# A delta-rule attention and mixer kernel: two of the eight transfers of the first K unit issued by GpSimd as its first instructions

## The chip, the cores and the metric

The kernel runs on one core of a Trainium2 chip. A core has TensorE (PE, matrix products, results in PSUM), VectorE (DVE), ScalarE (ACT), GpSimd (POOL) and SyncE (SP), which here only issues transfers. ScalarE and GpSimd issue transfers too. All transfers between the device's memory and the on-chip memory (SBUF) are carried by 16 DMA engines. The metric is the device time of one execution in microseconds (us); the smaller the better.

## The reference

Inputs are q, k, v of shape (4, 8, 768, 48), that is batch, heads, sequence and head dimension, beta of shape (4, 8, 768), and the mixer's weights U (768, 32), V (32, 768), w_ch1 (384, 1536) and w_ch2 (1536, 384), all float32. First a delta rule runs over the sequence, for each batch and head:

```
k_n = k / (norm(k) + 1e-6);  state = 0
for t: y[t] = q[t] @ state
       state += beta[t] * outer(k_n[t], v[t] - k_n[t] @ state)
```

Then the heads are laid side by side as x (4, 768, 384), and a mixer follows: `u = x + (x^T U V)^T`, `out = u + relu(u @ w_ch1) @ w_ch2`.

## The kernel before

The recurrence is cut into chunks of 64 steps. A *unit* is half of one batch's sequence for all 8 heads, 6 chunks each; there are 8 units. Within a chunk the rule becomes a triangular system built from the products of K with itself (Gram products), the norms of K and beta. A unit is worked as follows: K is loaded into a *slot* of SBUF (two slots, used in turn), TensorE turns it (line 233), ScalarE and VectorE copy it from PSUM (432 and 434 for the first unit, 437 for later ones), TensorE makes the Gram products (461), these are copied into the slot (473, 476, 480), VectorE lays their diagonal blocks out (521), ScalarE takes the square root for the norms (394, after loading a table), VectorE combines norms and beta (397 to 406) and then substitutes in a long series of small operations (530, 532). After that come the states and the outputs of the attention, and then the mixer, whose large matrix products (1264, 1358) take most of the kernel's time. Mixer weights are loaded and combined during the first units (858, 877, 883, 886).

The order of the work on all engines is written out by hand. Each part of the work is a Python generator that yields what it needs and which engine it uses next; `begin` numbers the parts in the order they are begun, and the string ORDER lists those numbers: each token lets one part issue its next step. Parts 0 and 1 are the two calls of `load` for the K of unit 0, 2 and 37 and such are further loads. Part 0 issues on SP the four heads of lower number, part 1 on ScalarE the four of higher number; within each part the transfers go by `s` = 0 to 3. A pair of `s` (0 and 1, then 2 and 3) forms one *half* j of the heads, and each half is turned by TensorE in one go once all of its four transfers have landed. One transfer is 64 x 6 pieces of 192 bytes, 72 KB.

An engine works its instructions in their order; a waiting instruction holds up all that stand behind it. Waits are set by the framework from what the instructions read and write. Transfers carry semaphores of their own, eight for those of SP and ScalarE together and eight for those of GpSimd, which are handed out in turn; so a transfer waits until the one eight before it in that group has landed.

Ahead of the ordered part the kernel sets up constants. On GpSimd these are the identity (`ident`, used by every turn on TensorE), a triangular mask (`upper`, `mask_u`) and two memsets of parts of the slots (275). Behind them on GpSimd's queue come, in this order: one Q transfer, two K transfers of unit 1, the two transfers of beta (363), the mixer's U (858), and more of K and Q. Beta is turned by TensorE at line 374 and copied by ScalarE at 378; in TensorE's order line 374 stands behind the Gram products of unit 0 and ahead of the turn of unit 1's K, and in ScalarE's order the copy of that turn (437) stands ahead of the table load and the square root of unit 0's norms (394).

Of the kernel before, what the change touches and what calls it, by code (L numbers as in the profile page):

```python
# [6 lines left out]
FP32 = mybir.dt.float32  # L7
# [16 lines left out]
def kernel(ctx: ExitStack, tc: tile.TileContext, q: bass.AP, k: bass.AP, v: bass.AP, beta: bass.AP, moe_U: bass.AP, moe_V: bass.AP, moe_w_ch1: bass.AP, moe_w_ch2: bass.AP, out: bass.AP):  # L24
# [59 lines left out]
    297 71 207 61 297 301 208 61 297 301 61 61 208 298.2 297 303 298 207 68 304q 208 298 70 71 304 44 207  # L84
# [1367 lines left out]
```

## Time and profile before

| | |
|---|---|
| median of 3 runs | 576.2 us (574.73 to 580.31) |
| the profiled execution | 572.55 us |
| its span | 570.8 us |
| granted TensorE clock, mean | 0.976 |
| TensorE busy | 537.4 us, 94% of the span |
| VectorE busy | 417.4 us, 73% |
| ScalarE busy | 243.1 us, 43% |
| GpSimd busy | 130.0 us, 23% |
| mean transfer rate over the span | 68 GB/s |

The span is the profiled execution without 1.75 us around it. Busy times of engines lie beside each other and do not add up to the span. "SPq", "ACTq" and "DVEq" are the sequencers that issue, an issue of a transfer by GpSimd counts as busy POOL. A row of the timeline has the start, the length, the engine, the line, the operation, what it writes and reads, how often, and in brackets the idle time before it and what ended that. A row of transfers has what is moved, the issuing queue, the count, the size, and the median time from issue to landing.

### The profile page before, as it was taken

Reading aid. Unit: us, or ns where it says so; the run is one execution under the profiler, and the core shown is the slowest. Engines: PE = TensorE matmul, PEld = TensorE weight load, DVE = VectorE, ACT = ScalarE, POOL = GpSimd, SP = SyncE. Lnnn points to the kernel's source line nnn. Section 1 sums busy time; section 2 is a strip of 40 time slices with the busy share of each in tenths; the row PEclk is TensorE's granted clock in tenths of the full one; section 3 lists DMA queues with packets and bytes.
Section 4 is the critical chain, followed back from the end, with each engine's and each line's share of the span. In section 5 each row is a group of like instructions: output and inputs, shape, how many; then the busy total and the mean of one; then the engine's idle time right before and its main releaser. Section 6 shows DMA issues by size and latency. Waiting matters only on the chain.

```text
span 570.8 us, 24657 instructions
## 1 busy us (share of the span) xinstructions
PE 537.4 (94%) x10965; PEld 454.7 (80%) x10965; DVE 417.4 (73%) x1062; ACT 243.1 (43%) x525; POOL 130.0 (23%) x229
## 2 busy tenths in 40 slices
PE   4776989999999999999999999999999999999997
PEld 4675877669789688789879977988879888656997
DVE  5798976799897439999887889999653356656542
ACT  3786885452435453155236433632452341336100
POOL 8061064552201453131044133400000000000000
PEclk9997579999999999999999999999999999999999
DMA  9957766542200353250033233310000000100001
GB/s 144 184 124 224 229 179 138 117 100 53 72 3 17 78 126 85 53 103 3 3 78 83 66 86 64 81 27 2 17 4 2 31 2 1 41 2 0 15 14 57
DMA packets 70763, 38.67 MB, mean 68 GB/s; under 512 B 56768, under 2 KB 67776, under 8 KB 70656
## 3 DMA queue, kind: packets, MB, share of 16 engines
q1 hardware_dynamic: 62368, 25.87, 19.2%
q0 software_dynamic: 6688, 10.92, 8.2%
q8 instruction: 86, 1.41, 1.1%
q10 hardware_dynamic: 1600, 0.30, 0.3%
q14 instruction: 21, 0.17, 0.1%
HBM read 32.34 MB, written 4.72 MB: 65 GB/s over the span
## 4 chain that ended last, share of the span: by engine, by line
PE 82%; DVE 8%; ACT 3%; DMA 2%; SPq 2%; issue 2%; DVEq 0%; ACTq 0%
PE P L1358 26%; PE P L1264 14%; PE P L221 9%; PE P L997 7%; PE P L461 4%; PE P L1041 2%; PE P L1088 2%; PE P L780 2%; PE P L739 2%; PE P L752 2%; DMA slot<-in_k_dram 2%; PE P L1186 2%; PE P L687 1%; PE P L1060 1%; PE P L694 1%
## 5 line engine op out<-in xcount | busy, mean ns | idle before, releaser
L1264 PE MATMUL P<-ut,w_sb 128*128 128x256 f32 x360 | 83.1, 385 | 0.2 <-ACT hs L1234 0.2
L1358 PE MATMUL P<-w_sb,hs 128*128 128x192 f32 x456 | 80.4, 330 | 0.0
L1358 PEld LDWEIGHTS P<-w_sb,hs 128*128 128x128 f32 x456 | 73.9, 190 | 3.9 <-issue 1.8
L1264 PEld LDWEIGHTS P<-ut,w_sb 128*128 128x128 f32 x360 | 66.7, 190 | 9.6 <-ACT hs L1234 0.3
L532 DVE TENSOR_TENSOR xt<-xt,prod 128x112 f32<-128x112 f32 (+21 forms) x200 | 64.2, 321 | 5.1
L530 DVE TENSOR_TENSOR prod<-gs,xt 128x112 f32<-128x112 f32 (+21 forms) x200 | 63.7, 318 | 4.3
L1304 DVE TENSOR_TENSOR X<-X,P 128x192 f32<-128x192 f32 x85 | 29.4, 347 | 42.9 <-PE P L1358 42.1
L344 POOL DMA_DIRECT2D slot<-in_k_dram x48 | 27.7, 582 | 95.5 <-PE P L780 60.9
L1234 ACT ACTIVATE hs<-P 128x512 f32<-128x512 f32 x42 | 24.9, 598 | 56.2 <-PE P L1264 43.6
L677 ACT COPY X<-P 64x192 f32<-64x192 f32 x96 | 30.1, 313 | 35.1 <-PE P L694 30.4
L1358 PE MATMUL P<-w_sb,S 128*128 128x192 f32 x240 | 41.3, 328 | 0.0
L1358 PEld LDWEIGHTS P<-w_sb,S 128*128 128x128 f32 x240 | 39.0, 190 | 0.8 <-DVE X L1304 0.6
L221 PE MATMUL P<-ut,w_sb 64*64 64x256 f32 x576 | 39.0, 383 | 0.2
L653 ACT COPY slot<-zz 32x384 f32<-32x384 f32 x64 | 34.5, 540 | 8.4 <-DVE zz L536 5.4
L461 PE MATMUL P<-slot 48*64 48x64 f32 x1536 | 33.1, 243 | 4.0 <-ACT slot L437 3.0
L461 PEld LDWEIGHTS P<-slot 48*64 48x64 f32 x1536 | 30.3, 156 | 7.4 <-ACT slot L437 3.6
L344 POOL DMA_DIRECT2D slot<-in_q_dram x48 | 27.2, 572 | 32.7 <-DVE slot L450 14.4
L657 POOL MEMSET slot<- 32x384 f32 x32 | 13.8, 431 | 90.9 <-PE P L628 89.8
L788 DVE TENSOR_TENSOR s<-s,P 128x192 f32<-128x192 f32 x40 | 14.0, 351 | 22.6 <-PE P L780 16.3
L982 DVE TENSOR_TENSOR slot<-slot,P 128x384 f32<-128x384 f32 x36 | 18.6, 551 | 15.8 <-PE P L997 15.5
L1358 PE MATMUL P<-w_sb,slot 128*128 128x192 f32 x180 | 29.9, 326 | 0.0
L1358 PEld LDWEIGHTS P<-w_sb,slot 128*128 128x128 f32 x180 | 29.4, 190 | 0.3
(205 smaller groups left out, 1059.1 us busy)
## 6 DMA issues: line engine op xcount, KB each, us to landing
w_sb<-in_moe_w_ch_dram SPq DMA_DIRECT2D x14, 384.0 KB, 5.2
out_dram<-X SPq DMA_DIRECT2D x22, 192.0 KB, 2.8
slot<-in_k_dram SPq DMA_DIRECT2D x36, 72.0 KB, 3.7
slot<-in_k_dram POOLq DMA_DIRECT2D x32, 72.0 KB, 3.3
slot<-in_v_dram SPq DMA_DIRECT2D x32, 72.0 KB, 3.0
slot<-in_v_dram POOLq DMA_DIRECT2D x32, 72.0 KB, 2.7
X<-in_moe_w_ch_dram SPq DMA_DIRECT2D x6, 384.0 KB, 4.6
wide<-in_moe_w_ch_dram SPq DMA_DIRECT2D x4, 384.0 KB, 5.8
```

The lines of the kernel that those rows point to most:

```text
L221: nc.tensor.matmul(to[half(g)], w[half(r), half(g)], x[half(r)], start=start, stop=stop, skip_group_check=True)
L344: queue.dma_start(out=in_pairs(n, int(name == 'q'), j)[quarter(2 * par + y), :, g, 0:cols.stop - cols.start], in_=of[:, :, cols])
L461: nc.tensor.matmul(p_g[half(g ^ par * i), par, c], kq[rows, c, j, 0, half(g)], kq[rows, c, j, i, half(g)], start=True, stop=True)
L530: nc.vector.tensor_tensor(out=prod, in0=gb[:, :, j, j + 1:, None].to_broadcast([128, split, w, m]), in1=xb[:, :, j:j + 1, 0:m].to_broadcas ...
L532: nc.vector.tensor_tensor(out=xb[:, :, j + 1:, 0:m], in0=xb[:, :, j + 1:, 0:m], in1=prod, op=ALU.subtract)
L653: nc.scalar.copy(pg[quarter(i), :, at, :, a:a + BK], thirds(h)[quarter(i)].rearrange('p r (c j) t -> p r c j t', j=2))
L677: nc.scalar.copy(x[half(c % 2), c // 2, 4 * D * g:4 * D * (g + 1)].rearrange('p (j r d) -> p r j d', r=2, d=D), states(p_y)[half(g)])
L997: nc.tensor.matmul(banks[x], w1_sb[:, 4 * a[0] + e, a[1]] if isinstance(a, tuple) else w1_mixes[a][:, e], tokens(*t) if isinstance(t, tupl ...
L1234: nc.scalar.activation(hs[:, fs[0]:fs[1] + 1:fs[1] - fs[0]], p_f, ACTF.Relu)
L1264: nc.tensor.matmul(p_f[:, x], w(x, t), ut[:, t], start=t == 0, stop=t == KT - 1)
L1304: nc.vector.tensor_tensor(out=to, in0=to, in1=p, op=ALU.add)
L1358: nc.tensor.matmul(to, of[0], of[1], start=of[2], stop=of[3], skip_group_check=True)
```

## The change

The tiles of the slots are made before the constants, and GpSimd issues two transfers ahead of everything else it does: `s` = 3 of both groups of heads, the last head of each group of four for unit 0's K. In `load`, unit 0's K skips `s` = 3, and the second half counts as issued as soon as `s` = 2 is. So SP and ScalarE issue three transfers each rather than four. The new helper `fetch` only holds the call of the transfer that stood in `load` before. In ORDER the two tokens of the removed steps are gone; all its other tokens are the same, in other line breaks. The order of the instructions on TensorE and VectorE is the same as before.

```diff
     ORDER = """
-    0 1 0 149 1 0 1 22 0 1 37 37 21 2 36 2 2 14.0 36 147 36 37 21 216 216 39 38 22 15.1 38 39 148 37 217.2
+    0 1 0 149 1 0 1 22 37 37 21 2 36 2 2 14.0 36 147 36 37 21 216 216 39 38 22 15.1 38 39 148 37 217.2 36 218
...
     def quarter(i, size=BK):
         return slice(BK * i, BK * i + size)
+    slots = [const.tile([128, 9792], FP32, name=f'slot{i}') for i in range(2)]
+
+    def fetch(queue, t, n, name, h):
+        b, hf = divmod(n, NU)
+        queue.dma_start(out=t, in_=name[b, h, hf * UC * L:(hf + 1) * UC * L, :].rearrange('(c t) d -> t c d', t=L))
+    for g in range(2):
+        fetch(nc.gpsimd, slots[0][half(g), 0:1536].rearrange('p (c s d) -> p c s d', c=UC, s=4)[:, :, 3, 0:D], 0, k, 4 * g + 3)
     ident = const.tile([128, 128], FP32, name='ident')
     make_identity(nc, ident)
...
-    slots = [const.tile([128, 9792], FP32, name=f'slot{i}') for i in range(2)]
...
             for s in range(1, 4, 2) if name == 'z' else range(4):
+                if (n, name, s) == (0, 'k', 3):
+                    emitted((name, n, g, 1))
+                    continue
                 to = dict(k=s, q=s, v=s % 2 * 2 + s // 2, z=s // 2)[name]
                 yield op(e)
-                queue.dma_start(out=t[half(1 - g if name == 'z' or (name == 'k' and n >= NU and s % 2) else g), :, to, 0:D], in_=src[b, 4 * g + s, hf * UC * L:(hf + 1) * UC * L, :].rearrange('(c t) d -> t c d', t=L))
+                fetch(queue, t[half(1 - g if name == 'z' or (name == 'k' and n >= NU and s % 2) else g), :, to, 0:D], n, src, 4 * g + s)
```

More of the change, by code (lines that the diff above doesn't have):

```diff
@@ new lines @@
+    337 205 206 9 9.0 349 350.1 205 206 348 9 9.0 206 205 348 338q 348 9 205 206 338 9.2 338 338 9 338 351.0 9.2
+    352 350 9 162 350 339q 350 9.2 339 9 351 339 9.1 80 89 90 89 90 89 90 89 90 81 81 80 80 339 351 87 9 90 9.2
+    336 339 90 9 89 334.1 90 334 356 9.2 89 90 357 340 9 89 351 83 334 357 355.2 83 9.0 91 92 340 9 89 92 91 92
+    341 359 88 91 334 88 87 9.0 355 354.1 9 88 87 9.0 341 9 84 354 84 354 357 210 209 355 342 355 354 210 209
+    354 333 342 92 210 360.0 363 9.2 353.1 361 9 9.2 344q 353 9 353 364 9.2 353 344 353 85 360 9 365.1 344 9.2
@@ new lines @@
+    360 344 360 9 78 78 364 9.0 344 9 78 364 9.2 366.0 343 365 9 9.2 365 365 368 207 208 9 78 367 9.1 208 207 78
+    369.2 78 85 345q 207 208 208 207 345 85 85 88 91 85 9 85 209 9.1 345 85 345 85 9 209 85 85 366 85 9.1 85 345
+    366 9 366 85 85 372.0 9.1 370 369 9 85 9.1 85 346 9 85 369 85 369 371 85 372 107 97 107 106 107 106 107 106
+    106 97 97 362.1 373 106 107 372 85 372 85 358.2 210 106 85 362 107 106 180.0 362 107 106 85 87 107 85 85 346
+    85 180 85 85 85 180.1 85 347 180 85 375 358 180.0 358 376 98 180 181.1 85 374.2 85 377q 98 181 104 377 388.0
[6 rows of a table added]
@@ new lines @@
+    102 102 391 387 391 102 409 102 10.0 410 182q.2 10 102 10.0 394 411 10 394 182 102 102 411 102 102 102 422.0
+    423 102 408.1 10.2 102 412q 10 102 10.2 102 422 412 10 422 102 10.2 422 102 424.0 10 412 102 10.2 408 412
+    408 10 102 412 102 10.1 426.2 425 424 10 102 10.1 424 413q 102 424 10 102 10.0 102 413 209 210 10 102 10.1
[7 rows of a table added]
+    449 119 10 10.0 450 446 440 450 451q 446 10 446 119 119 10.1 451 119 10 119 462.0 119 10.2 451 119 451 10
+    119 119 10.1 119 462 451 119 10 447.2 119 464 119 10.1 119 112 452 10 119 119 447 447 452 119 119 119 463.1
@@ new lines @@
+    465 10.2 119 453 119 462 462 119 119 10 453 119 119 10.0 466 468.2 463 10 119 10.0 463 454q 463 119 10 467
+    10.1 119 454 211 212 10 119 10.0 454 468 211 212 469.1 10 468 162 10.0 212 376 468 454 10 162 211 212 10.2
+    119 454 409 10 119 471.0 211 470 10.2 119 469 119 455 119 119 119 455 119 10 119 456 119 472 119 469 119 469
+    456 119 119 119 10.2 119 473 119 10 119 471 141 141 141 140 141 140 131 140 140 131 458q 471 132 471 132
+    183.1 474 467 119 119 131 458 183 140 141 119 183.2 162 141 140 458 458 119 141 138 183 138 141 458 119 138
@@ new lines @@
+    139 119 183q.0 119 140 139 474 119 138 139 478 183 184.1 474 476.2 140 139 119 119 475.0 477 476 119 119 476
[3 rows of a table added]
+    490 142 121 136 481.2 136 142 501 481 136 491 136 481 136 481 136 483 136 491 136 136 136 136 184q.0 136 136
+    486.2 129 184 492 486 502 162 486 492 136 129 493 503 136 136 493 504 504 504 11.1 505 136 494 11 136 136
+    136 494 136 136 136 495 136 136 136 11.0 506.2 136 495 506 136 506 11 136 136 11.1 508 136 510.2 185.0 11
+    507 11.1 509 497 11 185 136 136 136 11.1 136 497 509 136 136 11 511 11.0 512 513.1 510 11 509 11.0 510 498q
@@ new lines @@
+    136 11 496 510 11.0 498 136 11 136 11.2 136 514.0 498 513 136 498 136 513 513 11 136 11.1 136 498 11 136 136
+    11.2 136 185.1 11 136 515 11.2 136 185 514 11 499 516 514 136 514 136 136 136 136 136 499 136 518 136 523
+    522 500 519 522 519 522 522 11.2 524 523.1 11 523 517.0 523 522 11.2 525q 522 11 525 536.1 11.2 525 525 11
+    521 520 11.2 525 11 517 11.2 537 536 214 213 213 213 520 526q 214 517 517 214 526 214 536 214 536 521.0 214
+    521 213 526 520 526 214 520 520 214 520 11 526 521 521.1 521 538 11.2 539.0 521 527q 11 521 11.2 527 11 11.1
@@ L157 @@
+    527 527 11 11.2 527 11 540.1 214 11.2 213 541 539 214 539 528 214 539 214 542 542 528 542 529 543 11 529 530
+    544 530 532 545 532 547 546 546 546 533 531 548 533 549 11.0 550 523.2 11 523 11.0 523 540 534q 11 523 540
+    540 11.0 534 11 551.2 11.1 534 534 11 11.0 534 11 213 11.1 552.0 554 11 554 11.1 551 11 551 553 11.1 551 552
+    555.2 11 552 552 11.1 11 11.0 535q 11 556.1 11.0 535 11 11.0 555 558 11 557 556 213 558 215.0 215 566 556
[12 rows of a table added]
     """
```

30 lines of the change are left out of this document (2 added, 28 removed), and 136 rows, old and new, of the table ORDER.

## The prediction

> **What bounds the kernel now.** I read the page first: the share of each engine and the chain that ended last. Then the chain in order of time for the first 20 us, since the change touches only the start; then the timeline and the landings of the single transfers there.
>
> ```profile
> span 570.8 us, 24657 instructions
> PE 537.4 (94%) x10965; PEld 454.7 (80%) x10965; DVE 417.4 (73%) x1062; ACT 243.1 (43%) x525; POOL 130.0 (23%) x229
> PE 82%; DVE 8%; ACT 3%; DMA 2%; SPq 2%; issue 2%; DVEq 0%; ACTq 0%
> 18.00:42.00 24.00, 18.28 (x535) 16.52 (x538) 22.90 (x72) 18.97 (x38) 9.57 (x14) 1.00 0.68 151
> ```
>
> TensorE is busy 94% of the span and is 82% of the chain. A change of two transfers alters none of its work; it can only move the moment from which everything runs. The last row (columns: stretch, length, busy time and count of PE, PEld, DVE, ACT, POOL, then clock, DMA share, GB/s) says whether a move of the start is passed on: from 18 to 42 us VectorE is busy 22.90 of 24 us with the substitution, which starts when the norms are ready. There is no slack there, so a shift of the norms is a shift of what follows. The question is therefore when the norm of line 394 can run.
>
> ```profile
> 1.61 0.86 SPq L351
> ...
> 2.53 0.64 SPq L351
> ...
> 3.21 4.68 DMA slot<-in_k_dram
> 7.89 0.14 issue
> 8.02 1.00 PE P L233 x12
> 9.02 2.81 PE P L461 x96
> ...
> 13.26 0.80 ACT slot L480
> 14.06 0.79 ACT slot L437
> ...
> 14.87 1.28 ACT L394
> ...
> 16.16 0.26 ACT norm L394
> ...
> 18.07 0.13 DVE xt L406
> ```
>
> This chain (start, length, what) runs over SP's issues to the last transfer of the first unit's K (issued at 3.21, landed at 7.89) over its second turn on TensorE (8.02), the Gram products, their copies and the table load to the norm at 16.16, and on to the seed of the substitution (line 406). Taken by itself it says that K earlier by x makes the norm earlier by x. The timeline shows a second path that ends at the same place.
>
> ```profile
> 5.58 1.00 PE L233 MATMUL P<-ident,slot 64*128 64x64 f32 x12 [5.58 <-DVE even L283]
> ...
> 11.72 1.46 PE L374 MATMUL P<-ident,X 16*64 16x16 f32 x24
> ...
> 13.11 0.91 PE L233 MATMUL P<-ident,slot 64*128 64x64 f32 x12
> ...
> 14.05 0.80 ACT L437 COPY slot<-P 128x768 f32<-128x768 f32 x1
> ```
>
> The copy of line 437 stands ahead of the norm's table load on ScalarE. It reads the turn of the other slot's K, which TensorE ends at 13.11 + 0.91 = 14.02, and TensorE does that only after the turn of beta (line 374, 11.72 to 13.1). So line 437 is released at 14.02 by TensorE and at 14.06 by ScalarE: two paths within 0.04 us. The beta path hangs on two transfers of GpSimd's queue, and the change puts two others ahead of them.
>
> **The change part by part.** The order of the instructions on TensorE and VectorE is the same in both kernels; SP and ScalarE each issue three K transfers in place of four, GpSimd issues two more ahead of all its work.
>
> ```profile
> 0.83 3.01 SPq L351 DMA_DIRECT2D slot<-in_k_dram  x4
> 0.83 2.73 ACTq L351 DMA_DIRECT2D slot<-in_k_dram  x4
> ...
> 2.82 0.78 POOL L351 DMA_DIRECT2D slot<-in_q_dram  x1
> ...
> 3.60 1.31 POOL L351 DMA_DIRECT2D slot<-in_k_dram  x2
> ...
> 4.90 1.20 POOL L363 DMA_DIRECT2D X<-in_beta_dram  x2
> ```
>
> and what else on ScalarE and GpSimd could feel it:
>
> ```profile
> 1.25 0.29 POOL masks.py:199 TENSOR_SCALAR_AFFINE_SELECT ident<-ident 128x128 f32<-128x128 f32 x1
> ...
> 3.65 1.28 ACT L432 ACT_TABLE_LOAD   x1 [3.65 <-DVE slot L273]
> ...
> 6.54 0.48 ACT L432 COPY slot<-P 128x384 f32<-128x384 f32 x1 [1.61 <-PE P L233]
> ...
> 14.38 1.00 POOL L516 MEMSET xt<- 128x1056 f32 x1
> ```
>
> *Removed from ScalarE:* one issue of 2.73 / 4 = 0.68 us. It gains nothing: after its issues ScalarE waits until 3.65 for a memset of VectorE, loads a table, and needs that only at 6.54.
>
> *Removed from SP:* one issue of 3.01 / 4 = 0.75 us. SP's following transfers (Q, the other slot's K) are issued some 0.7 us earlier. They also lose a wait: the kernel's framework hands out eight semaphores in turn to the transfers of SP and ScalarE, so that SP's fourth and fifth now find a free one. These transfers are not needed before 13 us; what they do is to bring more work to the DMA engines sooner.
>
> *K's second half.* The landings, each from the one issue in its row and its median time:
>
> ```profile
> slot<-in_k_dram SPq DMA_DIRECT2D x1, 72.0 KB, 3.8
> slot<-in_k_dram SPq DMA_DIRECT2D x1, 72.0 KB, 4.1
> slot<-in_k_dram ACTq DMA_DIRECT2D x1, 72.0 KB, 4.4
> slot<-in_q_dram POOLq DMA_DIRECT2D x1, 72.0 KB, 3.8
> slot<-in_k_dram POOLq DMA_DIRECT2D x1, 72.0 KB, 4.8
> X<-in_beta_dram POOLq DMA_DIRECT2D x1, 48.0 KB, 5.1
> X<-in_beta_dram POOLq DMA_DIRECT2D x1, 48.0 KB, 5.8
> ```
>
> With the issue times 1.61, 2.53 (SP's second and third), about 2.9 (ScalarE's fourth), 2.82 (GpSimd's Q), 4.25 (its second K), 4.90 and 5.51 (beta), they landed at 5.4, 6.6, 7.3, 6.6, 9.05, 10.0 and 11.3; SP's fourth at 7.89 stands above. The first half of K is thus complete at 5.4, which is what released the first turn at 5.58 (VectorE's memset named there is only the nearest event). Between 5.4 and 7.89 five transfers of 72 KB landed: the four of the second half and GpSimd's Q between them, 0.5 us each. With K alone in the queues it is four: 5.4 + 4 x 0.5 = 7.4; and the third queue starts at the beginning rather than at 2.82, which may fill time that two queues left. I take 7.2, a gain of 0.7 us. Bounds: nothing (7.89, if GpSimd's transfers need as long as all others), and 1.44 us, since the first turn ends at 6.58 and the second could follow it at once in place of 8.02. The first half pays a little, as three queues now share: up to two transfers, 1.0 us, later. Its turn would then end at 7.6 and the second follow at once, still a gain of 0.4.
>
> *Moved on GpSimd:* all its work, by 0.78 + 0.66 us less the 0.12 by which its first issue is dearer than others, so 1.3 us. Of this, the identity (before ready at about 1.5) and the masks and memsets have time until 5.58 and later: nothing. The memset of the substitution's matrix, begun at 14.38 and 1.0 long, is needed at 18.07 (line 406): nothing, up to a shift of 2.7. Q and the other slot's K: needed behind beta. Beta is left.
>
> ```profile
> 11.59 0.66 POOL L351 DMA_DIRECT2D slot<-in_q_dram  x1 [0.66 <-DMA X<-in_beta_dram]
> ```
>
> This issue waited until 11.59 for the second beta transfer, which agrees with 11.3 and says that beta is late already: TensorE needed it at 11.72, a slack of 0.4 us less the 0.13 from a landing to its matmul. In the changed kernel the second beta transfer is issued at 6.8 rather than 5.51. Bounds of its landing: 11.3, if the DMA engines were the only limit and had made up all of it (they have the same bytes to move ahead of it, and begin sooner), and 12.6, if the whole 1.3 us stays. For the first speaks that the queues hold 5 us of work by then, so that issue time counts little; for the second that in GpSimd's own queue Q follows later, and that SP has one transfer more in front by its 0.7 us. From Q's landing (6.6) to the second beta's (11.3) GpSimd's queue took 4.7 us for four transfers; if Q follows K's last by one turn of it, at 7.3, that gives 12.0, and I take that.
>
> *The sum.* Without beta the norm comes 0.7 us earlier. With beta at 12.0 the turn of line 374 starts at 12.13 rather than 11.72: +0.4. Line 233 follows (0.91), line 437 starts at 14.46, the norm at 16.57. The gain of K turns into a wait of TensorE between lines 461 and 374. So +0.4 us: 572.55 + 0.4 = 573.0 for the profiled execution. The median of the runs shown is 576.2, 3.65 above the profiled one; the forecast is **576.6 us**, no change that a measurement can tell. About 1%, 5.8 us, is what one could tell here: three runs already lie 5.6 us apart.
>
> *Two rules against the change.* The Trainium skill, page "DMA: Bandwidth & Descriptors", section "Issuing engines are not separate DMA queues", says that all issuing engines feed the same 16 DMA engines and a further issuer saves only its issue time. The landings 0.5 us apart from three queues agree. By the rule alone K would gain just the transfer that no longer stands between, 0.5 us in place of 0.7; the sum would stay, as beta decides it. The other rule is the fourth rival.
>
> **The rivals.**
> 1. *Faster: beta comes in time.* If it lands by 11.0, TensorE goes on as soon as the Gram products end (11.1), and all of K's 0.7 us counts: 575.5. For it: same bytes, earlier start. Against it: it must land 0.3 us earlier than before though issued 1.3 later.
> 2. *Slower: beta carries the whole shift.* It decides from a landing after 12.13 on, in place of 11.3. At 12.6, line 374 starts at 12.75: +1.0, 577.2. For it: GpSimd's queue is first in first out, with two transfers of 72 KB more in it. Against it: those leave the other queues, and it starts 2 us sooner.
> 3. *The change does not do what it says:* GpSimd's K lands no sooner than SP's did (its quickest row here is 3.8 us after issue). The second turn stays at 8.02, or somewhat later; beta decides all the same: 576.6.
> 4. *GpSimd's issues are held up by VectorE.*
>
> ```profile
> 1.33 1.76 DVE L271 MEMSET P<- 128x2048 f32 x1 [1.33 <-PEq L1436]
> ...
> 3.17 0.38 DVE L273 MEMSET slot<- 128x384 f32 x1
> ```
>
> The new issues, from 0.83 to 2.27, fall under a long memset that ends at 3.09. Were they held until then, beta would be 0.8 us later than forecast: +1.2, 577.4. Against it: the two issues at 3.60 lie under VectorE's memsets of the slots and take 0.66 us each, the same as the one at 11.59. The Trainium skill has such a rule on the page "SBUF — State Buffer", section "Who interferes with whom": a VectorE instruction in a two-port mode shuts GpSimd out until it ends, and a transfer issued there starves. This trace does not show it for these memsets.
>
> There is one more uncertainty, which belongs to no rival:
>
> ```profile
> 50.50:77.80 27.30, 22.21 (x719) 20.43 (x720) 21.76 (x59) 21.90 (x47) 3.47 (x7) 0.50 0.77 240
> 85.00:120.00 35.00, 33.19 (x888) 24.40 (x888) 26.57 (x62) 15.58 (x32) 17.15 (x30) 1.00 0.53 120
> ```
>
> TensorE's clock is at half for one stretch of 27.3 us, which ends just before TensorE becomes the bound. If it fell some microseconds later or came twice, several microseconds would be lost; I see nothing in the change that does it.
>
> **How the numbers follow.** Forecast 0.48; rival 1 0.17, rival 2 0.20, rival 3 0.07, rival 4 0.05, anything else 0.03. No case reaches 5.8 us; the odds outside 1% come from the last and from the scatter of the runs: faster 0.04, same 0.91, slower 0.05. The cases lie between -1.44 (the bound of K's gain, with beta in time) and +1.9 (rivals 2 and 4 together: 1.0 + 0.8, rounded up). The run times scatter more than that, so the range goes from the lowest run less 1.44, 573.3, to the median plus 1.9 plus half the way to the highest run (2.1), 580.2.
>
> **What would show it.** In the changed profile: K's second half complete near 7.2 and the second turn at 7.2 to 7.6 rather than 8.02; line 461 ending near 11.1; then TensorE idle up to about 1 us before line 374, put down to the transfer of beta; line 437 near 14.5 and the norm near 16.6. Line 374 right behind line 461, with no idle time, means rival 1. GpSimd issues longer than 0.8 us at the start mean rival 4. The forecast of no change is wrong if the distance from the norm to the end, 554.6 us now, moves by more than about 2 us.

## The result, and the profile after

The changed kernel takes 579.33 us (median of 18 runs, 577.47 to 581.92), the kernel before 575.51 beside it (18 runs, 572.58 to 580.42). The ratio is 1.0058, with an interval of 1.0032 to 1.0084: slower by 0.6%, 3.3 us by the ratio (the two medians are 3.8 apart). That is a small but real loss where the forecast had +0.4 us. The spread of the two is different: none of the 18 changed runs is below 577.4; of the 18 before, 12 are at most 576.56 and 6 are at least 578.2, with none between. The upper six of the kernel before lie where all runs of the changed one do.

The page of the changed kernel: the span, the engines, and the chain's shares.

```profile
span 578.0 us, 24659 instructions
PE 543.2 (94%) x10965; PEld 458.3 (79%) x10965; DVE 417.2 (72%) x1062; ACT 243.1 (42%) x525; POOL 131.3 (23%) x231
PE 80%; DVE 8%; ACT 3%; DMA 3%; issue 2%; POOL 1%; SPq 1%; DVEq 0%; ACTq 0%; POOLq 0%
```

Of the stretches (columns as in the prediction) those that the prediction showed:

```profile
18.00:42.00 24.00, 18.21 (x491) 16.44 (x491) 22.90 (x73) 18.51 (x38) 9.19 (x14) 1.00 0.67 145
52.30:79.60 27.30, 23.09 (x720) 20.67 (x720) 21.93 (x60) 22.13 (x46) 3.46 (x6) 0.50 0.77 231
85.00:120.00 35.00, 30.98 (x841) 23.82 (x840) 22.89 (x50) 15.39 (x31) 16.37 (x29) 0.95 0.52 118
```

VectorE and ScalarE do the same work as before. TensorE is busy 5.8 us longer, and in the last row it is busy 31.0 of 35 us where it was 33.2, at a mean clock of 0.95 where it was 1.00. The long stretch at half clock lies elsewhere by 1.8 us and is as long as it was. So most of the loss is not at the start but between 85 and 120 us. I take the two places in turn.

**The start.** First the chain that ended last, for the first 20 us; then the timeline, both of the changed kernel.

```profile
0.72 0.64 issue
1.36 0.51 POOL slot L246
...
6.76 0.62 POOL X L368
7.38 5.24 DMA X<-in_beta_dram
...
12.66 1.46 PE P L379 x22
...
17.11 0.26 ACT norm L399
...
17.83 0.56 DVE norm L402
```

```profile
5.97 2.00 PE L229 MATMUL P<-ident,slot 64*128 64x64 f32 x24 [5.97 <-DMA slot<-in_k_dram]
7.90 2.84 PE L466 MATMUL P<-slot 48*64 48x64 f32 x96
...
12.04 0.39 PE L379 MATMUL P<-ident,X 16*64 16x16 f32 x2 [1.30 <-DMA X<-in_beta_dram]
...
17.35 1.00 POOL L521 MEMSET xt<- 128x1056 f32 x1
```

The change does to K what it says, and more. Both turns run as one row of 24 products from 5.97 on; its second half begins at 6.98, where the second turn began at 8.02. The chain no longer runs over K: it runs over GpSimd, whose first issue began only at 1.36 (0.64 us of "issue" stand before it; SP's first issue began at 0.83), so the second transfer of beta was issued at 7.38 rather than 5.51 and landed at 7.38 + 5.24 = 12.62. TensorE waits for beta, and the norm runs at 17.11 rather than 16.16: +0.95 us.

A second loss follows. GpSimd's memset of the substitution's matrix has slid from 14.38 to 17.35 and now lies under VectorE's first operation on the norms. The timeline of the kernel before has that operation as

```profile
16.88 0.14 DVE L397 TENSOR_SCALAR norm<-norm 128x32 f32<-128x32 f32 x1
```

so it took 0.14 us alone and takes 0.56 beside the memset, ending at 18.39, just after the memset's end at 18.35. With it the substitution begins 1.3 us late (line 530 at 19.40, line 525 at 18.10 before). This part is not the same in each run: in a second profile of the changed kernel the norm came at 17.56, the memset was over at 18.20, the operation began at 18.28 and took 0.14 us, and the substitution began at 19.49. Operation by operation, VectorE is 1.3 us late until 40 us and 1.2 at 51; at 53 us, where line 877 waits for a transfer of mixer weights that landed only 0.5 us later than before, the delay falls to 0.5. TensorE is 0.8 us late just before the second place.

**The race at 82 us.** Here K and Q of a later unit come in in pieces (line 344, 346 after the change, of 48 to 72 KB) from GpSimd and SP; VectorE transposes K (450, 455 after) and between those steps takes mixer weights apart (877, 883, 886; 882, 888, 891 after). SP issues the last two weight transfers of that time (858, 863 after), 384 KB each. GpSimd's last piece of K and SP's weights are issued at about the same time. The timeline of the kernel before:

```profile
78.17 1.13 POOL L344 DMA_DIRECT2D slot<-in_q_dram  x2
79.00 0.69 DVE L877 TENSOR_SCALAR power<-X 128x768 int32<-128x768 int32 x1
79.61 0.85 DVE L883 TENSOR_SCALAR X<-X 128x768 int32<-128x768 int32 x1
82.67 0.69 POOL L344 DMA_DIRECT2D slot<-in_k_dram  x1
82.80 1.21 SPq L858 DMA_DIRECT2D X<-in_moe_w_ch_dram  x2
86.35 1.04 DVE L450 STREAM_TRANSPOSE slot<-slot 128x384 f32<-128x384 f32 x2
```

and of the changed one:

```profile
79.18 1.43 POOL L346 DMA_DIRECT2D slot<-in_q_dram  x2
79.93 0.54 DVE L882 TENSOR_SCALAR power<-X 128x768 int32<-128x768 int32 x1
80.39 0.57 DVE L888 TENSOR_SCALAR X<-X 128x768 int32<-128x768 int32 x1
82.39 1.50 POOL L346 DMA_DIRECT2D slot<-in_k_dram  x2
83.20 0.56 DVE L882 TENSOR_SCALAR power<-wide 128x768 int32<-128x768 int32 x1
83.33 1.21 SPq L863 DMA_DIRECT2D X<-in_moe_w_ch_dram  x2
84.29 0.68 POOL L346 DMA_DIRECT2D slot<-in_k_dram  x1
90.55 1.04 DVE L455 STREAM_TRANSPOSE slot<-slot 128x384 f32<-128x384 f32 x2 [3.68 <-DMA slot<-in_q_dram]
92.54 0.45 PE L692 MATMUL P<-s,slot 48*64 48x48 f32 x16 [2.21 <-DVE z L775]
```

Before, the piece of K was issued at 82.67, 0.13 us ahead of the weights. After, it is issued at 84.29, 0.96 us behind them. The rows of that one transfer (median us to landing at the end), before:

```profile
slot<-in_k_dram POOLq DMA_DIRECT2D x1, 48.0 KB, 3.4
```

and after:

```profile
slot<-in_k_dram POOLq DMA_DIRECT2D x1, 48.0 KB, 6.0
```

It lands at 90.3 instead of 86.1, VectorE waits 3.68 us for it (the transfer that the row names is the one that landed nearest), and TensorE then 2.21 us for VectorE. After this pause TensorE runs 3.4 us at half clock:

```profile
93.20:96.60 3.40, 3.40 (x9) 2.68 (x10) 3.25 (x6) 1.35 (x2) 1.78 (x3) 0.51 0.73 158
```

(nine products in 3.4 us; the same stretch before held 104, smaller ones among them, at a clock of 1.00). TensorE is 0.8 us late until 89 us, 3.2 behind its wait, and 4.9 when the mixer's products of line 1358 begin (line 1363 at 129.94, line 1358 at 125.04 before). From there to the end it takes 448.1 us instead of 445.8, with another 3.4 us of half clock at 455 us, in which the kernels do not differ. So this pair of profiles is 7.2 us apart: 0.8 from the start, 2.4 from the race, 1.7 from the half clock behind it, 2.3 at the end; the medians of the runs are 3.8 apart.

**Why the order turned.** From GpSimd's first piece of K in this sequence (75.46 before, 76.40 after) to its last piece it takes 7.2 us before and 7.9 after; from that same first piece to SP's weights it takes 7.34 us before and 6.93 after. The two events that were 0.13 us apart have moved by 0.68 and by 0.41 against each other, and neither is a matter of the late start, which is taken out of both numbers. Both come from what GpSimd and VectorE do between 78 and 84 us.

*GpSimd is held after the change.* The second issue of the pair at 78.17 took 0.57 us, that of the pair at 79.18 took 1.43 - 0.57 = 0.87, and the second of the pair at 82.39 took 0.94. Each of the long ones ends 0.13 us after VectorE's operation on line 882 has ended (79.93 + 0.54 = 80.47, and the issue at 79.18 + 1.43 = 80.61; 83.76 and 83.89): GpSimd is held until that operation is done. In the kernel before, the operation began 0.27 us after the issue, and the issue went through; in the changed one it begins 0.19 us after it.

*VectorE was held before the change.* There GpSimd got through first and its memset came in between: lines 877 and 883 took 0.69 and 0.85 us, from 79.00 to 80.46. After, the same two take 0.54 and 0.57, from 79.93 to 80.96, 0.43 us less. SP's weights wait for VectorE to free their buffer (they are issued 0.05 us after the end of a small memset of VectorE there, in both kernels), and so they are issued 0.41 us sooner. Whichever of the two engines gets in first at this place delays the other, and both delays work on the race.

The 0.07 us by which GpSimd comes later against VectorE are its own. The rows of its wait instructions (ns min/median/max, first and last start us), between its second and fourth issue of this sequence, before, with the row of the third and fourth issue above (the third is the long one, 829 ns):

```profile
L344 POOL DMA_DIRECT2D slot<-in_k_dram x2: 572/700/829, 76.8 to 77.6; - x2
...
L344 POOLq EVENT_SEMAPHORE  x1: 42/42/42, 76.7 to 76.7; - x1
```

and after:

```profile
L346 POOLq EVENT_SEMAPHORE  x1: 43/43/43, 78.0 to 78.0; - x1
```

Before, it stands ahead of the third issue (76.78), after, ahead of the fourth, which starts 0.06 us after the end of the third rather than at once. There are seven such instructions in the sequence in both kernels; which transfer one precedes depends on which of the eight semaphores it draws, and two more transfers at the start move that by two. That last sentence is inferred from the code; that the wait sits elsewhere, and that the issues behind it are held, is in the records.

The Trainium skill, page "SBUF — State Buffer", section "Who interferes with whom", says that VectorE and GpSimd share a pair of ports, locked for the whole of an instruction by whichever came first, and that a transfer issued by GpSimd can starve on it; it lists `tensor_scalar` among the operations that can take the pair. This trace agrees in both directions: the issues are held until 0.13 us after line 882 ends (0.87 and 0.94 us instead of 0.57), and the operation on the norms is held until GpSimd's memset ends (0.56 instead of 0.14). That these operations run in such a mode no row shows.

### The profile page after: what moved, and what is told of

Read it like the earlier page. It is cut to its first block, busy times and chain, and to the rows that moved or that the text cites. A ratio compares the mean times of both kernels' runs of the same rounds, so it can differ in the third digit from the quotient of the medians.

```text
span 578.0 us, 24659 instructions
## 1 busy us (share of the span) xinstructions
PE 543.2 (94%) x10965; PEld 458.3 (79%) x10965; DVE 417.2 (72%) x1062; ACT 243.1 (42%) x525; POOL 131.3 (23%) x231
## 4 chain that ended last, share of the span: by engine, by line
PE 80%; DVE 8%; ACT 3%; DMA 3%; issue 2%; POOL 1%; SPq 1%; DVEq 0%; ACTq 0%; POOLq 0%
PE P L1363 25%; PE P L1269 14%; PE P L217 9%; PE P L1002 7%; PE P L466 3%; PE P L1046 2%; PE P L1093 2%; PE P L785 2%; PE P L744 2%; PE P L757 2%; PE P L692 2%; PE P L1191 2%; PE P L1065 1%; PE P L699 1%; DVE prod L535 1%
## 5 line engine op out<-in xcount | busy, mean ns | idle before, releaser
L455 DVE STREAM_TRANSPOSE slot<-slot 128x384 f32<-128x384 f32 x48 | 25.9, 562 | 6.8 <-DMA slot<-in_q_dram 3.7
```

Of the source, the lines that this page charges most:

```text
L455: nc.vector.transpose(to, in_pairs(n, i, j)[:, :, :, D * u:D * u + BK])
```

## The experiments

Three theories were set against each other. *The race:* the loss comes from GpSimd's last piece of K falling behind SP's weights, whatever happens at the start. *The late start:* the loss comes from beta, and later events only carry it on. *Scatter:* the two profiles differ by chance, mostly in where the clock is at half. In the string ORDER, 202 issues the pieces of that K, 248 two of the memsets between them, 160 the weights, 2 is beta, 20 the memset of the substitution's matrix.

**The two kernels once more**, unchanged.

> The kernel before once more, for its profile alone. Three theories are tested in this group. Start: the loss is made in the first 20 us (beta turned 0.9 us later, the memset of the substitution's matrix later) and is passed on to the end. Race: most of the loss arises at 82 to 90 us, where GpSimd's last transfer of unit 2's K and SP's two weight transfers of 384 KB are issued within a microsecond of each other; before, GpSimd is first by 0.13 us (82.67 against 82.80) and its transfer lands after 3.4 us; after, it is behind (84.29 against 83.33), lands after 6.0 us, and VectorE waits 3.7 us. Scatter: the two profiles differ by chance, mostly in where TensorE's clock is at half. Race expects GpSimd's transfer ahead of SP's in a profile with a span near 571 us and behind it in one of 574 or more. Scatter expects the half-clock stretch of 27 us at another place than 50.5 us, and VectorE's line 450 without a long wait whatever the time. Start says nothing of this run.

> The changed kernel once more, for its profile alone. Start: the norm near 17.1 us again, and the same shift of about 1 us at every later point but for the clock. Race: VectorE's line 455 waits over 2 us for a transfer near 87 us again, with GpSimd's last piece of unit 2's K issued behind SP's weights. Scatter: the wait is gone, or the second and third stretch of half clock (93 and 455 us) are gone and the span is nearer 573 us.

The kernel before took 582.28 us this time, and lost the race, in just the way of the changed kernel. Its timeline:

```profile
78.09 1.50 POOL L344 DMA_DIRECT2D slot<-in_q_dram  x2
78.91 0.55 DVE L877 TENSOR_SCALAR power<-X 128x768 int32<-128x768 int32 x1
82.30 1.22 SPq L858 DMA_DIRECT2D X<-in_moe_w_ch_dram  x2
83.26 0.60 POOL L344 DMA_DIRECT2D slot<-in_k_dram  x1
89.67 1.04 DVE L450 STREAM_TRANSPOSE slot<-slot 128x384 f32<-128x384 f32 x2 [3.90 <-DMA slot<-in_q_dram]
```

The second issue of the first pair took 1.50 - 0.57 = 0.93 us; line 877 began 0.255 us after it, where it had been 0.265 in the first profile. The changed kernel took 582.10 us, with the same wait (3.8 us). So a hundredth of a microsecond decides the race in the kernel before. That its two groups of runs come from this is likely and not shown, as a run without a profile does not tell who won. Nor is the race all that made this run long: near its end TensorE is 9.7 us behind the first profile, of which 4.1 arose at this place and 4.5 around a further stretch of half clock at 112 us.

**The race alone lost, on the kernel before.** The piece of K goes behind two memsets and the weights; the start is that of before.

```diff
-27 248 251 202 167 250 46 160 250 146 160 251.0 46 250 250 251
+27 248 251 167 250 46 160 250 146 160 251.0 46 250 250 202 251
```

> The kernel before with one GpSimd transfer, the last piece of unit 2's K, issued behind two memsets rather than ahead of them, so some 1.7 us later and behind SP's two weight transfers; the start is that of the kernel before. Race: this transfer lands near 90 us, VectorE waits 2 to 4 us for it, and the time rises by 2 to 4 us over the kernel before, most of the change's 3.3 us (ratio 1.004 to 1.007). Start: no change, at most 0.5 us, since the first 20 us are the same. Scatter: no change.

Measured: 578.66 us (12 runs; 574.27 before), ratio 1.0065 (1.0034 to 1.0095). The profile of this kernel, page, timeline and waits:

```profile
span 573.8 us, 24657 instructions
```

```profile
82.38 1.21 SPq L858 DMA_DIRECT2D X<-in_moe_w_ch_dram  x2
83.49 0.59 POOL L344 DMA_DIRECT2D slot<-in_k_dram  x1
89.52 0.58 DVE L450 STREAM_TRANSPOSE slot<-slot 128x384 f32<-128x384 f32 x1 [3.54 <-DMA slot<-in_q_dram]
```

```profile
PE P L687 <- DVE z L770: 2.4, 1, 2.4
```

With the norm at 16.40, only 0.24 us later than before, moving one issue by a microsecond costs as much as the whole change; a ratio clear of 1 where nothing but this order is changed also speaks against scatter. The profiled execution took 575.5 us: it has TensorE's wait of 2.4 us but no half clock until the very end. TensorE goes there from 0.4 us ahead of the first profile of the kernel before to 2.2 us behind it, so the pause itself costs about 2.6 us. Eight of the twelve runs are above 577.5; what is added in them was not seen here, in the changed kernel's profile it was the clock.

**The race won, on the changed kernel.** GpSimd issues its pieces of K ahead of two memsets that stood between them; nothing else is moved.

```diff
-249.1 248 201 249 146 202 ... 249 27 248 251 202 167
+249.1 201 249 146 202 ... 249 27 251 202 248 248 167
```

> The changed kernel with GpSimd's pieces of unit 2's K issued ahead of two memsets that wait for TensorE, so that the last piece is issued before SP's two weight transfers. The start is that of the changed kernel. Race: the long wait of VectorE near 87 us is gone and the time falls by 2 to 4 us, to within 1 us of the kernel before (ratio 0.999 to 1.003). Start: no gain, the ratio stays near 1.006. Scatter: ratio anywhere, with no tie to the wait. If the two memsets are needed at once, TensorE waits for them instead, by up to 3 us; the profile would show that.

Measured: 575.39 us (12 runs; 574.27 before), ratio 1.0018 (1.0000 to 1.0037); none of the runs is above 577.2. Its timeline:

```profile
82.76 2.27 POOL L350 DMA_DIRECT2D slot<-in_k_dram  x4
84.92 1.21 SPq L867 DMA_DIRECT2D X<-in_moe_w_ch_dram  x2
88.60 1.03 DVE L459 STREAM_TRANSPOSE slot<-slot 128x384 f32<-128x384 f32 x2
```

The last of the four pieces was issued at 84.45, ahead of the weights, and landed 2.1 us later; VectorE does not wait. The race accounts for all of the change's loss but some 1 us (0 to 2), although the start is as late as in the changed kernel.

**The start repaired, race left alone.** First beta goes ahead on GpSimd's queue, then also the memset of the substitution's matrix.

```diff
-0 1 0 149 1 0 1 22 37 37 21 2 36 2 2 14.0 36
+0 1 0 149 1 0 1 2 2 2 22 37 37 21 36 14.0 36
```

> The changed kernel with the two transfers of beta issued by GpSimd right behind its masks, ahead of Q and the other slot's K, so about 2 us earlier (4.8 rather than 6.75 us). Start, for its share of about 1 us: beta lands before 11 us, line 379 follows line 466 without idle time, the norm comes at 15.5 to 16.3 us rather than 17.1 to 17.6. Two theories of the race: if it is the late start that lets GpSimd's piece of unit 2's K fall behind SP's weights, the race is won again about as often as in the kernel before and the ratio is 0.998 to 1.002; if it is lost for another reason (the order of GpSimd's queue up to there), the ratio stays at 1.003 to 1.005, with VectorE's long wait near 86 us.

```diff
-148 37 217.2 36 218 ... 148 19 219 20 220
+148 37 20 217.2 36 218 ... 148 19 219 220
```

> As after_beta, and GpSimd's first memset of the substitution's matrix ahead of four Q transfers that wait for semaphores. In the changed kernel this memset runs at 17.35 to 18.35 us, beside line 402 on VectorE, which takes 0.56 us there and 0.14 us in the kernel before. If the memset is what slows it, line 402 takes 0.14 us again and the combined step from norm to line 530 is 0.4 us shorter; where after_beta has the memset over by then, the two kernels do not differ. Ratio 0.997 to 1.002 by the late start, 1.003 to 1.005 by another reason.

Measured: 580.72 us for the first, ratio 1.0071 (1.0042 to 1.0099), and 579.66 for the second, 1.0060 (1.0027 to 1.0092), against 575.9 before. Nothing is won back; both ratios lie above the 1.003 to 1.005 that was expected for a race lost in any case, with intervals that reach down to it. In the first, beta landed at 10.4 and the norm came at 16.45, but the memset ran at 18.22 and held the substitution until 19.36. In the second, the start is earlier than in the kernel before. Its timeline:

```profile
17.76 0.69 DVE L534 TENSOR_TENSOR gs<-gs,cp 128x512 f32<-128x512 f32 x1
...
84.33 1.21 SPq L867 DMA_DIRECT2D X<-in_moe_w_ch_dram  x2
85.28 0.57 POOL L350 DMA_DIRECT2D slot<-in_k_dram  x1
92.06 0.58 DVE L459 STREAM_TRANSPOSE slot<-slot 128x384 f32<-128x384 f32 x1 [3.42 <-DMA slot<-in_q_dram]
```

The substitution begins at 17.76 (18.10 before), and the race is lost by the same 0.96 us. So repairing the start repairs nothing. But in this profile the gained time is gone again by 63 us, in pauses of TensorE:

```profile
48.57 0.56 PE L723 MATMUL P<-slot 64*64 64x48 f32 x10 [2.46 <-issue]
54.49 0.26 PE L636 MATMUL P<-zz,slot 32*32 32x32 f32 x1 [2.53 <-issue]
```

It waits there for nothing that the profile shows. Such pauses differ in length, and mostly in place, from profile to profile (the kernel with all three edits, below, has them at the same two lines, of 1.64 and 3.35 us); what they are stays open. GpSimd's sequence thus began at 77.40, 1.9 us later than in the kernel before, and this run alone does not clear the late start of losing the race. The next but one does.

**All three edits together**, on the changed kernel.

> All three repairs: beta first, the memset early, GpSimd's pieces of unit 2's K ahead of two memsets. If the start costs 1.0 us (after_won stood at 1.0018) and the change of K's transfers gains up to 0.7 us by itself, the ratio is 0.996 to 1.000. If the shift at the start does not reach the end at all, it stays at 1.002.

Measured: 575.90 us against 575.9, ratio 0.9990 (0.9961 to 1.0018). With race and start repaired, the change is worth nothing that can be measured, although the norm comes at 15.32 rather than 16.16.

**The late start alone, on the kernel before.** Beta's transfers go behind the mixer's U and a piece of K.

```diff
-22 0 1 37 37 21 2 36 2 2 14.0 36 147 36 37 21
+22 0 1 37 37 21 36 14.0 36 147 36 37 2 2 2 21
```

> The kernel before with the two transfers of beta issued behind two further transfers of GpSimd's queue (U and a piece of the other slot's K), so about 1.6 us later; K's own transfers are untouched. This makes the late start alone. The norm is expected at 17 to 18 us. If a late start is enough to lose the race, nearly all runs are at 577.5 or above, as with the changed kernel, and the ratio is 1.004 to 1.008; if not, the start alone costs what separates after_won from before_won at most, 0.5 to 2 us with the race lost in about the same part of the runs as in the kernel before (ratio 1.001 to 1.004).

Measured: 575.43 us against 573.93, ratio 1.0015 (0.9983 to 1.0046). Beta landed at 13.8, and the norm came at 18.29 (17 to 18 was expected), 2.1 us late, more than twice the delay of the changed kernel. By the ratio 0.9 us of that reaches the end; the interval allows nothing as well as all of it, and in the profile TensorE is still 1.8 us late at 100 us. Eleven of the twelve runs are at most 576.5 us. GpSimd's sequence began at 77.29, as late as with beta and memset ahead (77.40); yet the profile has the race won, by 0.15 us:

```profile
84.47 0.71 POOL L344 DMA_DIRECT2D slot<-in_k_dram  x1
84.62 1.21 SPq L858 DMA_DIRECT2D X<-in_moe_w_ch_dram  x2
```

**The weights out of the way, on the changed kernel.** SP's two weight transfers go behind four of its Q pieces (two tokens 160 moved behind `250 168 167 55`).

> The changed kernel with SP's last two weight transfers of 384 KB issued behind four Q transfers of unit 2 rather than ahead of them; GpSimd's order is that of the changed kernel. This takes away the other side of the race. If it is these weights that hold GpSimd's piece of unit 2's K back, the piece lands within 4 us of its issue, VectorE's long wait near 87 us is gone or under 1 us, and the ratio falls to 0.999 to 1.003, as in after_won. If GpSimd's own lateness is the cause, whatever SP moves, the wait stays over 2 us and the ratio near 1.006. The weights themselves come some 3 us later; if VectorE needed them at once, it would wait for them there, up to 2 us.

Measured: 578.69 us against 573.93, ratio 1.0074 (1.0039 to 1.0109). The edit missed its aim: SP issued those Q pieces early, at 80.2, and the weights at 83.08 and 83.68, still around the piece of K at 83.65, which needed 4.9 us; VectorE waited 1.8. The wait is half as long, and the ratio is the highest of all, where 0.999 to 1.003 was expected of a wait that is gone. In the profile (576.05 us, below the median) TensorE loses 1.3 us at this place and 2.3 us around a stretch of half clock at 109 us; what makes the median is open. So this run says little for or against either theory, beyond that the piece also suffers when only one of the two weight transfers is clearly ahead of it.

**The race secured on the kernel before**, alone (on two chips) and with beta ahead of all else of GpSimd's transfers.

```diff
-249.1 248 201 249 146 202 ... 249 27 248 251 202 167
+249.1 201 249 146 202 ... 249 27 251 202 248 248 167
```

> The kernel before with only GpSimd's pieces of unit 2's K ahead of the two memsets. The kernel before wins the race by 0.13 us in one profile and loses it by 1.0 us in another, which was 10 us longer, about half of that by stretches of half clock. If it loses the race in a part of its runs, this kernel is faster by 0.5 to 2 us (ratio 0.9965 to 0.999) and its runs scatter less. If the memsets matter as much, no change. Against after_won it gives the cost of the start alone, at a race that both win: 0.5 to 1.5 us expected.

> before_won once more, on the chip of this group, so that the others compare with it directly. It had the ratio 0.9961. If its gain is that the race is never lost, no run is above 577.5 us, and the ratio lies between 0.993 and 1.000, nearer 1 the less often the kernel before loses on this chip.

> before_won with the two transfers of beta issued by GpSimd right behind its masks (2.8 rather than 4.9 us); K's transfers as in the kernel before. K bounds the start there (second turn at 8.0 us), so at most the 0.3 us go that TensorE waits on beta; ratio 0.994 to 0.998, the same as before_won within the interval. after_beta_xt_won, with beta first too, stood at 0.999: if beta first is itself what makes TensorE's later pauses longer, this kernel is slower than before_won by 1 to 2 us.

Measured: 574.49 us against 575.9, ratio 0.9961 (0.9930 to 0.9992), with no run above 576.4; on the second chip 573.77 against 573.93, ratio 1.0001 (0.9969 to 1.0034). With beta ahead: 573.66, ratio 0.9998 (0.9969 to 1.0026), where 0.994 to 0.998 was expected. By the theory of the race such a version gains what the kernel before loses by losing it now and then: 14 of its 35 runs were at 577.4 or more beside the first of these, 7 of 35 beside the others, and none of 23 where it stood beside the two race experiments. These are not counts of lost races. Against what was expected, two of the twelve runs with the race secured on the second chip are above 577.5 (577.53 and 579.46); four of the twelve with the race lost by edit are at 575.5 or less; and the profile of the kernel before that lost the race at 582.28 us is from the chip of those 23 runs. No version was shown to be better than the kernel before on every chip.

**All profiles side by side.** From the instruction records of each: the norm; the lead of GpSimd's sixth issue in the sequence before VectorE's line 877 (or its counterpart) begins; that issue's length; how far the last piece of K is issued behind the first weights; its time to landing; VectorE's wait.

| kernel | ratio | norm | lead | issue | behind weights | landing | wait |
|---|---|---|---|---|---|---|---|
| before | | 16.16 | 0.265 | 0.57 | -0.13 | 3.4 | none |
| before, run again | | 16.28 | 0.255 | 0.94 | 0.96 | 6.1 | 3.9 |
| before, race lost by edit | 1.0065 | 16.40 | 0.261 | 0.57 | 1.11 | 5.8 | 3.5 |
| before, late start | 1.0015 | 18.29 | 0.271 | 0.57 | -0.15 | 3.4 | none |
| before, race secured | 0.9961 | 16.30 | 0.262 | 0.94 | -0.48 | 2.3 | none |
| the same, second chip | 1.0001 | 16.47 | 0.253 | 0.94 | -0.47 | 2.3 | none |
| the same, beta ahead | 0.9998 | 15.86 | 0.255 | 0.93 | -0.48 | 2.2 | none |
| after | 1.0058 | 17.11 | 0.194 | 0.87 | 0.96 | 6.0 | 3.7 |
| after, run again | | 17.56 | 0.204 | 0.88 | 0.97 | 6.4 | 3.8 |
| after, beta ahead | 1.0071 | 16.45 | 0.191 | 0.87 | 0.96 | 6.5 | 3.6 |
| after, beta and memset ahead | 1.0060 | 15.82 | 0.195 | 0.87 | 0.96 | 6.5 | 3.4 |
| after, weights late | 1.0074 | 16.91 | 0.222 | 0.90 | 0.57 | 4.9 | 1.8 |
| after, race secured | 1.0018 | 16.90 | 0.184 | 0.86 | -0.47 | 2.1 | none |
| after, all three edits | 0.9990 | 15.32 | 0.205 | 0.89 | -0.47 | 2.3 | none |

With a lead of 0.255 us or less the issue is always held, from 0.265 on never, and between them (0.261, 0.262) it goes either way. The seven kernels made from the one before lie at this edge, from 0.253 to 0.271. The seven made from the changed one, from 0.184 to 0.222, lie 0.03 to 0.07 below the lowest of these. Whether the issue is held shows no tie to the norm's time. Where it is held and the pieces keep their order, the race is lost. From the first piece of the sequence to SP's weights it is 7.33 or 7.34 us in the three kernels where it is not held, and 6.91 to 6.94 in the ten where it is and the weights are where they were. Where VectorE waits 3.4 us or more, the ratio is 1.0058 to 1.0071, where it does not wait, 0.9961 to 1.0018; the weights late, with 1.8 us and 1.0074, do not fit in between. Followed product by product against the first profile of the kernel before, TensorE loses 4.1 us between 89 and 93 us in the five profiles that lose the race and have the clock at half behind it, 2.6 us with the race lost by edit, 1.3 with the weights late, and at most 0.1 in the six others.

One more loss is apart from the race. In seven of the profiles (three made from the kernel before, four from the changed one) a stretch of half clock, of 3.4 to 6.8 us, begins between 106 and 116 us, and TensorE falls back by 2.3 to 4.5 us around it. Two of the seven have the race secured. One profile for each kernel does not tell how often it comes.

What is shown by experiment is that the race by itself makes a loss of this size, and that the late start neither loses the race nor makes more than a part of the loss (1 us, 0 to 2). That the wait instruction of 0.04 us, moved by one issue, is what takes the changed kernel below the edge is read from these records: all seven changed kernels have it ahead of the fourth issue, and none of the others. Counted from the first issue of the sequence, the third is held in all fourteen (0.82 to 0.84 us), the fourth starts at 2.14 us in the seven without and at 2.21 in the seven with this wait, and VectorE's operation at 3.52 to 3.56 in all. No kernel was run that moves this wait or VectorE's operation alone, so this link remains argued.

## Why the prediction was right or wrong

The forecast of no change within 1% came out, and 579.3 us lies in the range. But the loss is real, the sum said +0.4 us, and most of the 3.3 us came from a place that none of its terms looked at. That the time lies in the range is luck: without the 2.1 us that it added for the scatter of three runs, the range would end at 578.1, and a loss behind 80 us had at most the 0.03 of "anything else".

- **K's second half: right in kind, mis-sized.** The prediction took 7.2 for its landing and 0.7 us of gain; both turns followed each other and the gain was 8.02 - 6.98 = 1.04, between the 0.7 taken and the bound of 1.44. The Gram products ended at 7.90 + 2.84 = 10.7 rather than 11.1. As foretold, all of this became a wait for beta.
- **Beta: the step failed in its size.** It put the landing at 12.0, between 11.3 and 12.6; it was 12.62, the upper bound. That GpSimd's work moves by 1.3 us was too little by 0.5: the step counted the two issues from 0.83 on, and the first began at 1.36. So the second rival's case came true here, and at its price: +0.95 at the norm, against +1.0.
- **"The memset of the substitution's matrix ... nothing, up to a shift of 2.7": failed.** GpSimd's next issues wait for earlier transfers, so that the memset moved by 2.97 us, not by 1.3, into VectorE's operation on the norm. The step weighed only when its result is needed. It cost 1.30 - 0.95 = 0.35 us more at the substitution's start in this profile.
- **"A shift of the norms is a shift of what follows": failed in part.** The row of 18 to 42 us looked as foretold (22.90 us of VectorE), and the shift was passed on through it; but the wait for weights at 53 us took back 0.7 of it. The view ended at 42 us, and the next place with slack lay behind it. How much of a shift reaches the end stays open: a delay of 2.1 us at the norm cost the kernel before 0.15% (-0.17 to 0.46%), 0.9 us, and 1.8 us of it were left at 100 us in its profile.
- **The distance from the norm to the end: this is the term that failed.** The prediction named 554.6 us, and 2 us as what it could bear. It is 578.0 - 17.1 = 560.9 in the profile. The order of instructions on TensorE and VectorE was the same, as the prediction says, and it drew from this that only the start moves. What changed is GpSimd's timing against VectorE by 0.07 us, and through the two holds the order of two issues that stood 0.13 us apart.
- **The fourth rival had the mechanism and looked in the wrong place.** It asked whether VectorE holds up GpSimd's issues, checked that under the memsets of the first 4 us, found 0.66 us both ways, and closed with "this trace does not show it for these memsets". That holds for the start of the changed kernel too (0.66 us for the second issue). But the profile of before has an issue of 0.83 us where its neighbours take 0.57, the third of the sequence, at 76.78, under line 877. A search of all GpSimd issues for long ones would have shown this hold in the kernel before, and the two issues 0.13 us apart behind it.
- **The clock.** The prediction allowed that the half clock might come twice and "several microseconds would be lost", and saw nothing in the change to do it. The pause of TensorE at 90 us is such a thing: in the profiles of the changed kernel, of its second run and of the two with the start repaired, 3.4 us of half clock begin 1.7 to 3.1 us after VectorE goes on. It doesn't always come: the kernel with the race lost by edit had the pause without it.

## What to carry to other kernels

When an engine is given a little more to do at the start, what moves is not only its later work but the phase of its whole queue against the others; look through the trace of before for pairs of events on different queues that are a tenth of a microsecond apart and ask what happens if they change places. Runs of a kernel that fall into two groups can point to such a place, and a profile from each group is worth comparing. GpSimd issues and memsets that lie beside VectorE operations of the kinds that held them here need a margin of the length of that operation, and small transfers that are needed soon should go well ahead of large ones from another queue.

## What the runs showed of the hardware

- A GpSimd issue of 0.57 us is held until 0.13 us after the end of a VectorE bitwise operation on 128x768 integers (0.54 us) that begins within about 0.26 us of the issue's start: it takes 0.82 to 0.94 us where the operation begins 0.17 to 0.26 us after it. The same operation beginning 0.01 us later does not hold it. In the other direction, a small VectorE operation (0.14 us) that meets a GpSimd memset waits for the end of it (0.56 us).
- A transfer of 48 KB lands after 2.1 to 3.4 us when issued 0.1 to 0.5 us ahead of two transfers of 384 KB on another queue, and after 5.8 to 6.5 us when issued 1 us behind them.
- GpSimd's first issue began at 1.36 us, where SP's and ScalarE's began at 0.83 and 0.82. The profile shows no reason.
- After its pause of 2.2 us TensorE ran 3.4 us at half clock in the changed kernel's profile, and likewise in four others with the race lost (pauses of 2.1 to 2.4 us), not in the one with the race lost by edit (2.4 us).
- TensorE pauses of up to 3.4 us, most of them in the middle of a group of like products, for nothing that the profile shows, and mostly at other places in each profile. One place recurs: a pause of 0.4 to 1.2 us at line 461 or its counterpart between 104 and 113 us in nine profiles, in seven of which the clock is at half within the 3 us behind it; the five without a pause of that length have no half clock there.
